# Joining a weight word's low bits by an OR on VectorE, and a first gate step as a rectifier on ScalarE

## The chip, the cores and the metric

The kernel runs on one core of a Trainium2 chip. The metric is the device time of one execution in microseconds (us). A core has five engines that run side by side, each through its own instructions in order: TensorE (PE in the rows, with its weight loads as PEld), VectorE (DVE), ScalarE (ACT), GpSimd (POOL) and SyncE (SP), which issues most DMAs.

## The reference

An attention layer is followed by a feed-forward layer with a piecewise gate. For each of 8 batches and 8 heads (576 tokens, 64 channels):

```
out_d     = softmax(q_d k_d^T / 8) v_d          # q_d, k_d, v_d: means over groups of 4 tokens
out_local = softmax(q k^T / 8 where |i - j| < 4) v
x         = repeat(out_d, 4) + out_local        # 4608 tokens x 512
h         = x @ w_in                            # 512 -> 2048
g         = h where h >= 1, 0 where h <= -1, else (h + 1)^2 / 4
out       = g @ w_out                           # 2048 -> 512
```

The two weight matrices arrive as 64-bit floats: each weight is two 32-bit words, a high one and a low one.

## The kernel before, in words

**Numbers.** Each operand of the feed-forward products is held as two tiles in TensorE's fast 32-bit format: a rounded high part and the rest. A product is then three matmuls: high by high, low part of the weight by high, high by low part of the activations.

**Weights.** `w_in` and `w_out` are cut into 16 blocks each (`i0` to `i15`, `o0` to `o15`; 128 x 512 weights). The kernel makes single precision from the 64-bit words in six pieces per block, in the function `convert`. `c1` (L803, ACT) turns the high word in place: sign and exponent. `c3` (L816, DVE) shifts it left by three into a new tile `m`. `c2` brings down the top three bits of the low word: on ACT (L812) for 24 blocks, on DVE (L810) for the eight odd `o` blocks named in `ON_VECTOR`. `c4` (L819, DVE) adds these bits to `m`; this 32-bit integer addition is built as an instruction of its own that works on 1,024 16-bit halves. `c5` (L822, ACT) rounds `m` to the high part `w[:, 0]`, and `c6` (L826, POOL) subtracts that from `m` for the rest, `w[:, 1]`.

**Stages.** The first 512 tokens are chunk 0. While the first eight head pairs of the attention run, the weights are loaded and converted, and chunk 0 passes both products, all interleaved. From about 155 us on, the weights are there, and the other chunks (384 tokens, later 512) pass with the rest of the attention. The last two chunks use a Strassen scheme.

**Gate.** For a block `f` of 128 hidden channels, TensorE sums `h` in PSUM (`f.s0` to `f.s3`, L847; chunk 0 uses two PSUM banks in turn). The gate has five pieces. `u1` is max(h, -1) + 1 (L869, DVE; in chunk 0 it reads PSUM, later a copy `m` made by ACT at L868). `sq` is the square of half of it (L872, ACT). `u2` is min(max(h, 1), that square) (L875, DVE). `gh` rounds (L881, ACT) and `gl` is the rest (L884, POOL). `m{f}.0` to `m{f}.3` (L902) multiply `gh` and `gl` with block `o{f}` for four token groups.

**What sets the order.** In this first part no scheduler moves anything: the table `ORDER` is a written list of tokens (`i6.c4`, `f4.u1`, `m3.2`, `5.x`), and each engine gets its instructions in the order of these tokens. Tokens such as `5.x` are steps of head pair 5: `sl` and `sp` are the local and the pooled scores on TensorE (L311 to L323, L377), `mx` and `ms` the local maximum and its subtraction on DVE (L334, L353), `x` the sum of both attention outputs on DVE (L541). `x` reads the PSUM tile that the next pair's `sl` then writes. Tiles `m`, `u`, `gh` and `gl` share ten buffers (`temp`), so that a writer can wait for the reader of an old tile.

Of the kernel before, what the change touches and what calls it, by code (L numbers as in the profile page):

```python
# [11 lines left out]
I32 = mybir.dt.int32  # L12
U32 = mybir.dt.uint32
U8 = mybir.dt.uint8
AF = mybir.ActivationFunctionType
ALU = mybir.AluOpType
# [11 lines left out]
NFC = DFF // P  # L28
# [52 lines left out]


WARM = 10
ON_VECTOR = {("o", f) for f in range(1, NFC, 2)}

PIECES = (3, 4, 2, 1)

# [73 lines left out]
def attention_then_ffn(ctx: ExitStack, tc, qT, kT, vw, vp, vq, band, members, w_in, w_out, out):  # L161
    nc = tc.nc
# [625 lines left out]
    raw, weights = {}, {}  # L788
# [6 lines left out]
    def temp(name, kind=F32):  # L795
        return mpool.tile([P, 512], kind, name=name, tag="t512", bufs=10)

    def convert(name, f, piece):

        t = raw[name, f]  # L800
        if piece == 1:
            high = t.bitcast(F32)[:, :, 1]
            nc.scalar.activation(high, high, AF.Prelu, scale=2.0**-112, alpha=-(2.0**32))  # L803
        elif piece == 2:
            raw["low", name, f] = t[:, :, 0]
            if (name, f, "m") in raw and (name, f) not in ON_VECTOR:
                raw["low", name, f] = t.rearrange("p n t -> p (n t)")[:, 0:512]
            low = t.bitcast(U32)[:, :, 0]
            if (name, f) in ON_VECTOR:
                nc.vector.tensor_scalar(raw["low", name, f], low, 2.0**-29, None, op0=ALU.mult)  # L810
            else:
                nc.scalar.activation(raw["low", name, f], low, AF.Copy, scale=2.0**-29)  # L812
        elif piece == 3:
            raw[name, f, "m"] = temp("m")
            mi = raw[name, f, "m"].bitcast(I32)
            nc.vector.tensor_scalar(mi, t[:, :, 1], 3, None, op0=ALU.logical_shift_left)  # L816
        elif piece == 4:
            mi = raw[name, f, "m"].bitcast(I32)
            nc.vector.tensor_tensor(mi, mi, raw["low", name, f], op=ALU.add)  # L819
        elif piece == 5:  # L820
            w = wpool.tile([P, 2, 512], F32R, name=f"w_{name}{f}", tag=f"w{name}{f}")
            nc.scalar.copy(w[:, 0], raw[name, f, "m"])  # L822
            weights[name, f] = w
        else:
            w = weights[name, f]
            nc.gpsimd.tensor_tensor(w[:, 1], raw[name, f, "m"], w[:, 0], op=ALU.subtract)  # L826
# [5 lines left out]
    utiles = {}  # L832
# [25 lines left out]
    def gate(c, f, piece):  # L858

        size = CHUNKS[c][1]  # L860
        h = htiles.get((c, f))
        if piece == "u1":
            utiles[c, f] = temp("u")[:, :size]
            if (c, f) in summed:
                m = utiles["m"] = summed[c, f]
            elif c > 0:
                m = utiles["m"] = temp("m")[:, :size]
                utiles["copied"] = nc.scalar.copy(m, h)  # L868
            nc.vector.tensor_scalar(utiles[c, f], m if c > 0 else h, -1.0, 1.0, op0=ALU.max, op1=ALU.add)  # L869
        elif piece == "sq":  # L870
            u = utiles[c, f]
            nc.scalar.activation(u, u, AF.Square, scale=0.5)  # L872
        elif piece == "u2":
            u = utiles[c, f]
            utiles["last"] = nc.vector.scalar_tensor_tensor(  # L875
                u, utiles["m"] if c > 0 else h, 1.0, u, op0=ALU.max, op1=ALU.min
            )
        elif piece == "gh":
            gh, gl = (temp(x, F32R)[:, :size] for x in ("gh", "gl"))
            gtiles[c, f] = gh, gl  # L880
            nc.scalar.copy(gh, utiles[c, f])  # L881
        else:
            gh, gl = gtiles[c, f]
            nc.gpsimd.tensor_tensor(gl, utiles.pop((c, f)), gh, op=ALU.subtract)  # L884

    def gates(c, f, pieces=GATE):
        with tc.high_priority(offset=100):
            for piece in pieces:
                gate(c, f, piece)
# [170 lines left out]
    with psum("pair") as two, tc.manual_schedule(), ExitStack() as six:  # L1060
# [7 lines left out]
        for token in ORDER:  # L1068
            token, _, spare = token.partition("+")
            spare = int(spare or 0)  # L1070
            token, _, tag = token.partition("@")
            whose, what = token.split(".")
            kind, f = whose[0], whose[1:]
            if kind in "io":
                if what == "ld":
                    load_weights(kind, int(f))
                else:
                    convert(kind, int(f), int(what[1]))
            elif kind == "f":
                c, f = divmod(int(f), NFC)  # L1080
                if not banks:
                    six.close()
                    single(six, ["h0"], ["o0"], ["o1", "o2"], ["h1"], ["o3"])
                if what[1:].isdigit() and what[0] == "s":
                    keep_up(banks["o0"][:, 0:P], spare)
                    product(c, f, int(what[1]))
                else:
                    gate(c, f, what)
            elif kind == "m":
                second_product(0, int(f), int(what))  # L1090
            elif tag:
                ops[int(whose)][what](own[tag], tag, spare)
            elif spare:
                ops[int(whose)][what](spare)
            else:
                ops[int(whose)][what]()
# [162 lines left out]
```

## Time and profile before

| | |
|---|---|
| median of 3 runs | 897.67 us (896.5 to 898.2) |
| span of the profiled execution, from its first to its last instruction | 900.0 us |
| PE busy | 885.3 us (98%) |
| DVE busy | 563.7 us (63%) |
| ACT busy | 467.9 us (52%) |
| POOL busy | 375.0 us (42%) |
| PE's share of the chain that ended last | 84% |

The profiled execution is one more than the three timed ones; what is known of its own time is its span, 2.3 us above the median of the runs. Busy shares are means over the whole span; the stages differ, and a share says nothing of who waits for whom at a given moment. For that, idle time of an engine is listed with the instruction that ended it.

### The profile page before, as it was taken

The page shows a single profiled execution, that of the slowest core. Times are in us where ns is not written, and L with a number is a line of the kernel's source. Part 1 is how long each engine was busy: PE and PEld are TensorE (multiplying, and loading weights), DVE is VectorE, ACT ScalarE, POOL GpSimd, SP SyncE. Part 2 cuts the span into 40 slices and gives each one's busy share as a digit, 9 for nine tenths or more (in the row PEclk, how much of TensorE's full clock was granted, in tenths as well). Part 3 has the DMA queues.
Part 4 walks back from the last instruction along what each step waited for, and adds up shares of the span by engine and source line. Part 5 has one row for each costly group of instructions (what it writes and reads, how often), then busy time and mean ns, then how long its engine had stood idle before and what let it go on. Part 6 is the DMA issues. An engine that isn't in the chain of part 4 may idle for free.

```text
span 900.0 us, 19773 instructions
## 1 busy us (share of the span) xinstructions
PE 885.3 (98%) x7808; PEld 798.0 (89%) x7808; DVE 563.7 (63%) x1077; ACT 467.9 (52%) x1025; POOL 375.0 (42%) x361
## 2 busy tenths in 40 slices
PE   8999899999999999999999999999999999999998
PEld 6687688899999999999999999989999989999997
DVE  6699995766566477566556656665556546754442
ACT  4798675554544545554454454564454444434333
POOL 3166783444343244444432443344444434433232
PEclk9999999999999999999999999999999999999999
DMA  9369311333233233333332343342233212434341
GB/s 344 120 213 319 126 57 53 97 110 128 90 115 115 91 106 116 122 120 116 113 103 89 101 133 103 105 139 92 91 127 106 83 51 83 122 109 141 105 126 53
DMA packets 67884, 106.47 MB, mean 118 GB/s; under 512 B 5808, under 2 KB 33456, under 8 KB 67792
## 3 DMA queue, kind: packets, MB, share of 16 engines
q1 hardware_dynamic: 67648, 105.17, 35.5%
q8 instruction: 61, 1.00, 0.4%
q14 instruction: 31, 0.25, 0.1%
q10 hardware_dynamic: 144, 0.05, 0.0%
HBM read 71.51 MB, written 17.83 MB: 99 GB/s over the span
## 4 chain that ended last, share of the span: by engine, by line
PE 84%; DVE 7%; ACT 4%; issue 3%; POOL 2%; DMA 0%; SPq 0%; DVEq 0%; ACTq 0%; POOLq 0%
PE ffn_o L902 37%; PE ffn_h L847 28%; PE ffn_h L1015 7%; PE score_ps L643 2%; PE turn_ps L771 1%; PE value_ps L667 1%; DVE m L819 1%; PE local_ps L768 1%; PE value_ps L625 1%; DVE m L816 1%; DVE u L869 1%; DVE u L875 1%; POOL gl L884 1%; ACT u L872 1%; DVE sums L924 1%
## 5 line engine op out<-in xcount | busy, mean ns | idle before, releaser
L884 POOL TENSOR_TENSOR gl<-u,gh 128x384 fp32r<-128x384 f32 (+1 forms) x176 | 197.0, 1120 | 400.4 <-ACT gh L881 320.3
L902 PE MATMUL ffn_o<-w_o,gh 128*128 128x512 f32 x1152 | 347.5, 383 | 0.0
L847 PE MATMUL ffn_h<-xh,w_i 128*128 128x384 f32 (+1 forms) x1184 | 301.2, 336 | 2.5 <-POOL w_i L826 2.1
L902 PEld LDWEIGHTS ffn_o<-w_o,gh 128*128 128x128 f32 x1152 | 212.0, 190 | 25.2 <-issue 0.6
L847 PEld LDWEIGHTS ffn_h<-xh,w_i 128*128 128x128 f32 x1184 | 209.5, 189 | 16.9 <-POOL w_i L826 2.9
L902 PE MATMUL ffn_o<-w_o,gl 128*128 128x512 f32 x576 | 218.9, 380 | 0.4 <-POOL gl L884 0.4
L847 PE MATMUL ffn_h<-xl,w_i 128*128 128x384 f32 (+1 forms) x592 | 197.3, 333 | 0.0
L872 ACT ACTIVATE u<-u 128x384 f32<-128x384 f32 (+1 forms) x176 | 97.4, 553 | 133.5 <-DVE u L869 133.5
L881 ACT CAST gh<-u 128x384 fp32r<-128x384 f32 (+1 forms) x176 | 95.3, 542 | 118.8 <-DVE u L875 117.3
L869 DVE TENSOR_SCALAR u<-m 128x384 f32<-128x384 f32 (+1 forms) x160 | 76.1, 476 | 127.3 <-ACT m L868 126.9
L875 DVE SCALAR_TENSOR_TENSOR u<-m,u 128x384 f32<-128x384 f32 (+1 forms) x160 | 103.2, 645 | 78.0 <-ACT u L872 78.0
L902 PEld LDWEIGHTS ffn_o<-w_o,gl 128*128 128x128 f32 x576 | 109.3, 190 | 16.4 <-POOL gl L884 0.8
L847 PEld LDWEIGHTS ffn_h<-xl,w_i 128*128 128x128 f32 x592 | 111.9, 189 | 2.2
L868 ACT COPY m<-ffn_h 128x384 f32<-128x384 f32 (+1 forms) x132 | 63.8, 484 | 51.1 <-PE ffn_h L847 42.4
L720 ACT ACTIVATE sl<-sl 128x640 f32<-128x640 f32 x24 | 17.7, 739 | 55.1 <-POOL sl L694 55.1
L581 POOL TENSOR_TENSOR xl<-x,xh 128x576 fp32r<-128x576 f32 (+4 forms) x32 | 35.3, 1110 | 16.6 <-ACT xh L580 16.6
L826 POOL TENSOR_TENSOR w_o<-m,w_o 128x512 fp32r<-128x512 f32 x16 | 24.1, 1517 | 31.2 <-ACT w_o L822 31.2
L924 DVE SCALAR_TENSOR_TENSOR sums<-sums 128x128 f32<-128x128 f32 (+1 forms) x72 | 33.0, 459 | 1.6
L694 POOL TENSOR_TENSOR sl<-sl,mxl 128x640 f32<-128x640 f32 x24 | 30.2, 1260 | 2.3 <-DVE mxl L693 1.7
L924 DVE SCALAR_TENSOR_TENSOR words<-sums,words 128x512 fp32r<-128x512 f32 x16 | 17.7, 1109 | 17.7 <-ACT words L928 17.7
L826 POOL TENSOR_TENSOR w_i<-m,w_i 128x512 fp32r<-128x512 f32 x16 | 22.6, 1415 | 11.6 <-ACT w_i L822 11.4
L1041 POOL TENSOR_TENSOR m<-both 128x256 f32<-128x256 f32 x14 | 10.7, 765 | 39.0 <-DVE both L1040 33.8
(179 smaller groups left out, 1183.4 us busy)
## 6 DMA issues: line engine op xcount, KB each, us to landing
xh<-kept SPq DMA_DIRECT2D x56, 256.0 KB, 3.8
v<-vw SPq DMA_DIRECT2D x29, 320.0 KB, 4.0
vq_sb<-vq SPq DMA_DIRECT2D x24, 384.0 KB, 3.0
out<-osb SPq DMA_DIRECT2D x36, 256.0 KB, 2.4
raw_i<-w_in SPq DMA_DIRECT2D x16, 512.0 KB, 8.7
raw_o<-w_out SPq DMA_DIRECT2D x16, 512.0 KB, 8.9
kept<-words SPq DMA_DIRECT2D x32, 256.0 KB, 2.6
k_sb<-kT SPq DMA_DIRECT2D x28, 288.0 KB, 3.3
```

Of the source, the lines that this page charges most:

```text
L581: nc.gpsimd.tensor_tensor(xl[:, p, dst], x[:, part], xh[:, p, dst], op=ALU.subtract)
L826: nc.gpsimd.tensor_tensor(w[:, 1], raw[name, f, "m"], w[:, 0], op=ALU.subtract)
L847: ins = nc.tensor.matmul(htiles[c, f], wi[:, wt, cc * P : (cc + 1) * P], turns(xt[:, cc, ts]), start=(cc == 0 and xt is xh and wt == 0), s ...
L868: utiles["copied"] = nc.scalar.copy(m, h)
L869: nc.vector.tensor_scalar(utiles[c, f], m if c > 0 else h, -1.0, 1.0, op0=ALU.max, op1=ALU.add)
L872: nc.scalar.activation(u, u, AF.Square, scale=0.5)
L875: utiles["last"] = nc.vector.scalar_tensor_tensor(u, utiles["m"] if c > 0 else h, 1.0, u, op0=ALU.max, op1=ALU.min)
L881: nc.scalar.copy(gh, utiles[c, f])
L884: nc.gpsimd.tensor_tensor(gl, utiles.pop((c, f)), gh, op=ALU.subtract)
L902: ins = nc.tensor.matmul(o, gt[:, ts], turns(weights["o", f][:, wt, :]), start=f == 0 and n == 0, stop=f == NFC - 1 and n == 2,)
L924: return nc.vector.scalar_tensor_tensor(out, a, 1.0, b, op0=ALU.mult, op1=op)
L1015: ins = nc.tensor.matmul(ps, left(wt, k), right(xt, k), start=not more and k == 0 and wt == xt, stop=k == 1 and xt == 1, skip_group_check= ...
```

## The change

It touches `convert` and `gate` alone. Pieces `c2` and `c3` do nothing any more. In `c4`, a first DVE instruction multiplies the low word by 2 to the power -29 and caps the result at 7, into a new tile `m`. A second one shifts the high word left by three and ORs it with `m`. In chunk 0, `u1` becomes one ACT instruction, relu(h + 1), which reads PSUM. The table `ORDER` stays as it is, so the new instructions stand where the tokens `c4` and `u1` stand.

```
-ON_VECTOR = {("o", f) for f in range(1, NFC, 2)}
...
-        elif piece == 2:
-            raw["low", name, f] = t[:, :, 0]
-            if (name, f, "m") in raw and (name, f) not in ON_VECTOR:
-                raw["low", name, f] = t.rearrange("p n t -> p (n t)")[:, 0:512]
-            low = t.bitcast(U32)[:, :, 0]
-            if (name, f) in ON_VECTOR:
-                nc.vector.tensor_scalar(raw["low", name, f], low, 2.0**-29, None, op0=ALU.mult)
-            else:
-                nc.scalar.activation(raw["low", name, f], low, AF.Copy, scale=2.0**-29)
-        elif piece == 3:
+        elif piece in (2, 3):
+            return
+        elif piece == 4:
             raw[name, f, "m"] = temp("m")
             mi = raw[name, f, "m"].bitcast(I32)
-            nc.vector.tensor_scalar(mi, t[:, :, 1], 3, None, op0=ALU.logical_shift_left)
-        elif piece == 4:
-            mi = raw[name, f, "m"].bitcast(I32)
-            nc.vector.tensor_tensor(mi, mi, raw["low", name, f], op=ALU.add)
+            nc.vector.tensor_scalar(mi, t.bitcast(U32)[:, :, 0], 2.0**-29, 7.0, op0=ALU.mult, op1=ALU.min)
+            nc.vector.scalar_tensor_tensor(
+                mi, t[:, :, 1], 3, mi, op0=ALU.logical_shift_left, op1=ALU.bitwise_or
+            )
...
-            nc.vector.tensor_scalar(utiles[c, f], m if c > 0 else h, -1.0, 1.0, op0=ALU.max, op1=ALU.add)
+            if c == 0:
+                nc.scalar.activation(utiles[c, f], h, AF.Relu, bias=1.0)
+            else:
+                nc.vector.tensor_scalar(utiles[c, f], m, -1.0, 1.0, op0=ALU.max, op1=ALU.add)
```

Three places show what moves. The first is DVE around `i2.c4`, between the maximum (`mxl`) and the subtraction (`sl`) of pair 4; `raw_i2` is the loaded block, `m` the tile that is made of it. Before:

```order
L816 TENSOR_SCALAR m_591<-raw_i2_488 128x512
L556 TENSOR_TENSOR xl_70<-pl_ps_521,xh_69 128x64
L819 ISA m_396<-m_396,raw_i0_299 128x1024
L334 TENSOR_REDUCE mxl_648<-sl_ps_600 128x10
L819 ISA m_591<-m_591,raw_i2_488 128x1024
L353 TENSOR_TENSOR sl_674<-sl_ps_600,mxl_648 128x640
```

Now:

```order
L808 TENSOR_SCALAR m_591<-raw_i0_299 128x512
L809 SCALAR_TENSOR_TENSOR m_591<-raw_i0_299,m_591 128x512
L333 TENSOR_REDUCE mxl_641<-sl_ps_594 128x10
L808 TENSOR_SCALAR m_665<-raw_i2_485 128x512
L809 SCALAR_TENSOR_TENSOR m_665<-raw_i2_485,m_665 128x512
L352 TENSOR_TENSOR sl_669<-sl_ps_594,mxl_641 128x640
```

The first of the two instructions for `i2` has moved from ahead of the maximum to behind it, so two instructions now stand between maximum and subtraction instead of one.

The second place is ACT around `f4.u1`; `u_1015` is the gate tile of `f4`, `ffn_h0` its sum in PSUM, `w_o4` and `w_i6` are casts `c5` of two blocks. Before:

```order
L881 CAST gh_1013<-u_985 128x512
L803 ACTIVATE raw_i8_953<-raw_i8_953 128x512
L812 ACTIVATE raw_i6_828<-raw_i6_828 128x512
L822 CAST w_o4_1038<-m_889 128x512
L872 ACTIVATE u_1034<-u_1034 128x512
L812 ACTIVATE raw_o6_857<-raw_o6_857 128x512
L822 CAST w_i6_1053<-m_1021 128x512
```

Now:

```order
L876 CAST gh_997<-u_969 128x512
L802 ACTIVATE raw_i8_937<-raw_i8_937 128x512
L862 ACTIVATE u_1015<-ffn_h0_697 128x512
L814 CAST w_o4_1017<-m_1009 128x512
L867 ACTIVATE u_1015<-u_1015 128x512
L814 CAST w_i6_1035<-m_1025 128x512
```

The two low-word copies are gone, and the cast of `o4` now stands behind an instruction that needs TensorE's sum of `f4`.

The third place is ACT around `f7.u1`; `u_1229` is the gate tile of `f7`. Before:

```order
L822 CAST w_o8_1221<-m_1175 128x512
L822 CAST w_i10_1228<-m_1191 128x512
L822 CAST w_i9_1234<-m_1202 128x512
L822 CAST w_i8_1241<-m_1136 128x512
L803 ACTIVATE raw_o11_1189<-raw_o11_1189 128x512
L872 ACTIVATE u_1249<-u_1249 128x512
```

Now:

```order
L814 CAST w_o8_1197<-m_1184 128x512
L814 CAST w_i10_1208<-m_1191 128x512
L814 CAST w_i9_1214<-m_1199 128x512
L814 CAST w_i8_1221<-m_1205 128x512
L862 ACTIVATE u_1229<-ffn_h1_710 128x512
L802 ACTIVATE raw_o11_1165<-raw_o11_1165 128x512
L867 ACTIVATE u_1229<-u_1229 128x512
```

The first gate step of `f7` has moved from DVE to behind four casts on ACT, each of which needs a finished `m` from DVE.

## Rows read from the trace of the kernel before

**Rows 1.** Windows: length, busy time of each engine (instructions), granted clock, DMA share, GB/s.

```profile
50.00:100.00 50.00, 47.56 (x354) 39.45 (x352) 48.46 (x69) 45.10 (x78) 36.69 (x25) 1.00 0.62 213
...
250.00:300.00 50.00, 50.00 (x458) 46.05 (x457) 32.71 (x70) 24.41 (x57) 20.26 (x22) 1.00 0.32 104
```

**Rows 2.** Timeline of PE: start, time taken, instruction, idle before it with releaser.

```profile
43.64 0.71 PE L377 MATMUL sp_ps<-kd,first_qd 64*64 64x144 f32 x12 [1.19 <-DVE sl L353]
...
47.71 0.48 PE L847 MATMUL ffn_h<-xh,w_i 128*128 128x512 f32 x1 [0.36 <-POOL w_i L826]
...
68.43 0.38 PE L847 MATMUL ffn_h<-xl,w_i 128*128 128x512 f32 x1
...
75.52 0.48 PE L847 MATMUL ffn_h<-xh,w_i 128*128 128x512 f32 x1 [1.77 <-POOL w_i L826]
...
92.60 0.70 PE L847 MATMUL ffn_h<-xh,w_i 128*128 128x512 f32 x2 [0.29 <-DVE u L875]
...
101.88 0.55 PE L311 MATMUL sl_ps<-band_r,ident_r 128*128 128x384 f32 x2 [2.26 <-DVE x L541]
...
109.13 0.71 PE L377 MATMUL sp_ps<-kd,first_qd 64*64 64x144 f32 x12 [0.75 <-DVE sl L353]
...
121.25 0.48 PE L902 MATMUL ffn_o<-w_o,gl 128*128 128x512 f32 x1 [0.43 <-POOL gl L884]
```

**Rows 3.** Window behind the longest of these waits (columns as in rows 1).

```profile
103.00:107.00 4.00, 4.00 (x23) 3.24 (x17) 4.00 (x6) 3.48 (x7) 1.81 (x2) 0.57 0.55 154
```

**Rows 4.** Groups up to 185 us: count, busy us, mean ns of one, idle before.

```profile
L819 DVE CUSTOM_DVE_ANT_0 m<-m,raw_i 128x1024 uint16<-128x1024 uint16 x16 | 14.6, 926 | 2.3 <-ACT raw_i L812 2.3
...
L812 ACT ACTIVATE raw_i<-raw_i 128x512 int32<-128x512 uint32 x16 | 12.5, 797 | 0.0
L816 DVE TENSOR_SCALAR m<-raw_o 128x512 int32<-128x512 int32 x16 | 11.1, 707 | 0.0
...
L869 DVE TENSOR_SCALAR u<-ffn_h 128x512 f32<-128x512 f32 x16 | 11.0, 689 | 1.8 <-PE ffn_h L847 1.7
L816 DVE TENSOR_SCALAR m<-raw_i 128x512 int32<-128x512 int32 x16 | 10.7, 669 | 0.9 <-ACT raw_i L803 0.9
...
L819 DVE CUSTOM_DVE_ANT_0 m<-m,raw_o 128x1024 uint16<-128x1024 uint16 x8 | 8.1, 1012 | 0.4 <-ACT raw_o L812 0.4
L819 DVE CUSTOM_DVE_ANT_0 m<-raw_o,m 128x1024 uint16<-128x1024 uint16 x8 | 8.0, 997 | 0.0
L812 ACT ACTIVATE raw_o<-raw_o 128x512 int32<-128x512 uint32 x8 | 6.9, 864 | 1.1 <-DVE m L816 1.1
...
L810 DVE TENSOR_SCALAR raw_o<-raw_o 128x512 int32<-128x512 uint32 x8 | 6.2, 780 | 0.0
```

**Rows 5.** Single lines: durations in ns, least/median/most, first and last start.

```profile
L816 DVE TENSOR_SCALAR m<-raw_o x16: 420/514/1454, 27.7 to 131.4; 128x512 int32<-128x512 int32 x16
...
L869 DVE TENSOR_SCALAR u<-ffn_h x16: 672/680/742, 47.3 to 143.6; 128x512 f32<-128x512 f32 x16
...
L924 DVE SCALAR_TENSOR_TENSOR sums<-xh,xl x8: 676/681/693, 730.5 to 781.3; 128x512 f32<-128x512 f32 x8
...
L910 ACT COPY osb<-ffn_o x36: 577/587/602, 153.0 to 896.0; 128x512 f32<-128x512 f32 x36
```

**Rows 6.** Timeline of POOL around 72 us (columns as in rows 2).

```profile
70.05 1.98 POOL L826 TENSOR_TENSOR w_o<-m,w_o 128x512 fp32r<-128x512 f32 x1 [2.27 <-ACT w_o L822]
71.99 1.80 POOL L884 TENSOR_TENSOR gl<-u,gh 128x512 fp32r<-128x512 f32 x1
73.75 1.71 POOL L826 TENSOR_TENSOR w_i<-m,w_i 128x512 fp32r<-128x512 f32 x1
...
75.42 1.29 POOL L826 TENSOR_TENSOR w_o<-m,w_o 128x512 fp32r<-128x512 f32 x1
```

**Rows 7.** Timeline of DVE ahead of pair 5's `x` (columns as in rows 2).

```profile
97.90 1.85 DVE L819 CUSTOM_DVE_ANT_0 m<-raw_o,m 128x1024 uint16<-128x1024 uint16 x1
99.68 1.48 DVE L816 TENSOR_SCALAR m<-raw_i 128x512 int32<-128x512 int32 x1
```

## The prediction

> **What bounds the kernel now.** I read the windows first, then TensorE's own idle time, then the groups of instructions, then the timelines of single engines. The windows show two stages. From 155 us on PE is full: 50.00 of 50 us in the window shown, with DVE at 32.71 and ACT at 24.41 [rows 1]. Between 50 and 100 us all are near full: DVE 48.46, ACT 45.10, PE 47.56. The changed code runs in that early part only (the last of its instructions starts at 143.6 us, rows 5 show it for L869), so its worth is what PE loses there. Idle time of DVE or ACT is worth nothing by itself.
>
> PE's losses can be counted. Seven waits are left once the first products start: 1.19, 0.36, 1.77, 0.29, 2.26, 0.75 and 0.43 us, together 7.05 [rows 2]. Behind the longest, the granted clock falls from full to its lower level (2.4 to 1.2 GHz) for most of 103 to 107 us: a mean of 0.57, so 0.43 x 4 = 1.7 us more [rows 3]. PE had been idle for 2.26 us shortly before it fell. The ceiling of the gain is 7.05 + 1.7 = 8.8 us, 1% of the time, whatever the other engines save. As PE is full behind it, what is saved early should arrive at the end undiminished.
>
> **The engines' sums.** DVE loses 32 shifts (11.1 + 10.7), 32 additions (14.6 + 8.1 + 8.0), eight low-word products (6.2) and 16 gate steps (11.0): 69.7 us [rows 4]. It gains 32 low-word products with a cap and 32 shift-and-OR instructions. The first is priced as L810, same input and output kinds, 0.78 us. The second has no row of its own. Below, an undisturbed two-input instruction of its size takes 0.68 [rows 5]; above, one held up takes 1.85 [rows 7]. I take the mean of the additions it replaces, 30.7 / 32 = 0.96, since it stands in the same places beside the same POOL work. That is 32 x (0.78 + 0.96) = 55.7, so DVE is relieved of 14 us (24 us if every OR took 0.68; burdened by 14 more if every OR took 1.85). ACT loses 24 low-word copies, 12.5 + 6.9 = 19.4 us [rows 4], and gains 16 rectifiers from PSUM at 0.59, as L910 takes [rows 5]: 9.4. It is relieved of 10 us. POOL's list of work is unchanged, and so is PE's.
>
> **Wait by wait.** Fewer us do not mean an earlier start where an instruction waits in line, so each of PE's waits is followed to what ends last there.
>
> At 43.64 PE waits for pair 4's subtraction. The product for `i2` now stands between maximum and subtraction, which it did not: about 0.4 us (L816 undisturbed, rows 5) later. PE reaches its next wait, 47.71, that much later, and of the 0.36 there as much goes. Together a loss of 0.1. Nothing hides it, as there is no PE work between the two.
>
> At 75.52 PE waits for `i6.c6` on POOL, third in a row of three without a gap: `o4.c6`, `f3.gl`, `i6.c6`, begun at 70.05 when ACT had cast `o4` [rows 6]. That cast now stands behind `f4.u1`, which cannot start before PE ends `f4`: 68.43 + 0.38 = 68.81 [rows 2]. With 0.59 for the rectifier and an estimated 0.6 for the cast, an ACT instruction of the same size, POOL starts at 70.0. So ACT's relief is eaten here by its new wait, and behind the waiting rectifier stand the casts of `o4` and `i6`, on which POOL depends. What is left is that the three POOL instructions took 1.98, 1.80 and 1.71 where the next one took 1.29 [rows 6], while DVE's pairs for `o5` and `o6` still run beside them. I take 0.5 of the 1.77 (bounds 0 and 1.77).
>
> The rows show that DVE and POOL hold each other up: L816 takes 420 to 1,454 ns, L869, which reads PSUM, 672 to 742 [rows 5]. The Trainium skill (SBUF — State Buffer, section Who interferes with whom) says that a VectorE instruction with two SBUF inputs, or a one-input one in its two-port mode, and a GpSimd instruction that reads SBUF exclude each other for their whole length, and that one SBUF input outside that mode does not contend. By that rule the 16 gate steps that leave never disturbed POOL, and of the disturbing kind only 8 of 72 go. Then the 0.5 would be about 0, and the sum below 0.5 less; the rows fit the rule.
>
> At 92.60 PE waits for DVE's `f7.u2`. Its `u1` now stands on ACT behind four casts, which wait for five pairs of DVE instructions (`o7`, `o8`, `i10`, `i9`, `i8`). I take the wait to stay as it is, 0 gained: before, the same casts came ahead of `sq`.
>
> At 101.88 PE waits 2.26 us for pair 5's `x`, which came late because DVE was behind: the two instructions just ahead took 1.85 and 1.48 [rows 7]. By then DVE has been spared eight gate steps (5.5 us at 0.69), five L810 (3.9) and two shifts that had run ahead (1.4): some 10 us, of a delay of 2.26. What is late next is `x`'s own input from PE, and three quarters of a block of products lie between that and the wait. I take all 2.26, and with it the clock's 1.7 (bounds 0 and 4.0).
>
> At 109.13 PE waits for pair 6's subtraction; one gate step, one L810 and one shift (1.65 by a disturbed run) leave the stretch between that pair's scores and it. I take all 0.75. At 121.25 PE waits for a `gl`; POOL's work there stays, as do DVE's joins beside it: 0 (bounds -0.8 and 0.43).
>
> Sum: -0.1 + 0.5 + 0 + 2.26 + 1.7 + 0.75 + 0 = 5.1 us. The profiled execution would span 900.0 - 5.1 = 894.9; it stood 2.3 us above the median of the runs, 897.67. So I forecast 897.67 - 5.1 = 892.6 us.
>
> **The rivals.** (A) All waits go: the engines' relief carries everywhere, 8.8 - 0.1 = 8.7 us, 889.0. For it: the relief of DVE is larger than any wait. Against it: 75.52 hangs on ACT's place in line and on POOL.
>
> (B) No change to be measured: DVE stays late at `x` since its pairs are each held up, as the two in rows 7. Then 2.26 and 1.7 stay, and 0.75 + 0.5 - 0.1 = 1.2 us are saved: 896.5. For it: the number of disturbing instructions barely falls, and instructions that ran ahead as `c3` now run in pairs at `c4`, near their users.
>
> (C) Slower: the place is `f7.u1`. Five DVE pairs must end before ACT comes to it, then `sq`, `u2` and PE. At 1.74 us a pair (0.78 + 0.96) they take 8.7 us; at 3.33, the sum of rows 7, they take 16.7, and PE waits 8 us more at 92.60. From 1.74 + 5.1 / 5 = 2.8 us a pair on, the gain elsewhere is gone. At 3.33 it is 897.67 - 5.1 + 8.0 = 900.6. Against it: POOL's next casts come from these same five pairs, so it has little work with which to hold them up.
>
> (D) The OR is not one plain pass but takes as long as the slowest row. Were it 1.85 us each, DVE gains no time at all, which is C's cause or B's.
>
> **How the numbers follow.** Forecast with its own range of 890.5 to 895.5: 0.58. A: 0.12. B (895.5 to 899): 0.20, C with D: 0.10. The range runs from A's 889.0 up to 898.0, which leaves out C and the upper part of B. About 0.2%, 1.8 us, is what a measurement of this kernel can tell from no change: faster means under 895.9, slower above 899.5. Forecast, A and a tenth of B fall below: 0.58 + 0.12 + 0.02, and a little of C's small ends: 0.73. Same 0.17, slower 0.10.
>
> **What would show it.** Right: in the new trace PE's wait for `x` at about 99 us is gone and the clock there is full; PE still waits about 1 us for `i6.c6`, with the rectifier of `f4` starting only when PE ends that block; the products and ORs take 0.4 to 0.7 us alone. `sp` of pair 4 starts 0.3 to 0.4 us later than 43.64, and the window from 155 us on is a shifted copy. Wrong: a new PE wait behind a rectifier, above all at `f7` or `f9`; a PE idle time that brings the clock down at another place; or a gain of more than 8.8 us, for which nothing in the early waits has room.

## The result and the profile after

The changed kernel took 907.38 us (median of 5 runs, 905.39 to 908.47), the kernel before 897.67: a ratio of 1.0082, with an interval of 1.0056 to 1.0109. The forecast was 892.6, the range 889.0 to 898.0. The medians alone differ by 9.7 us, 1.1%; one of the five runs of the kernel before took 902.61. The change made the kernel slower by about 1%, and the prediction was wrong in size and in sign.

The profiled execution took 908.47 us, and its span is 906.6: 1.9 us lie around the span. TensorE (PE) is still the engine that is full (888.7 us busy, 98%). From the start of the 384-token chunk to the end both kernels take the same time: PE's first product of it starts at 144.00 us before and at 150.69 after, and the spans end 756.0 and 755.9 us later. So, as predicted, the difference was made in the first part. What follows is PE's idle time there, as [rows 2] show it before: the timeline of PE in the trace after, the waits of over 0.2 us from 40 us on (start, time taken, instruction, idle before it with releaser).

```profile
44.81 0.71 PE L376 MATMUL sp_ps<-kd,first_qd 64*64 64x144 f32 x12 [1.65 <-DVE sl L352]
...
55.69 0.82 PE L468 MATMUL tp_ps<-ident,sp 128*72 128x128 f32 x6 [0.49 <-DVE sp L419]
...
65.92 0.56 PE L310 MATMUL sl_ps<-band_r,ident_r 128*128 128x384 f32 x2 [0.82 <-DVE x L540]
...
77.21 0.48 PE L839 MATMUL ffn_h<-xh,w_i 128*128 128x512 f32 x1 [0.87 <-POOL w_i L818]
...
85.33 0.48 PE L839 MATMUL ffn_h<-xh,w_i 128*128 128x512 f32 x1 [0.30 <-ACT w_i L814]
...
86.69 0.48 PE L839 MATMUL ffn_h<-xh,w_i 128*128 128x512 f32 x1 [0.88 <-POOL w_i L818]
...
97.93 0.70 PE L839 MATMUL ffn_h<-xh,w_i 128*128 128x512 f32 x2 [2.21 <-DVE u L870]
...
145.66 0.70 PE L839 MATMUL ffn_h<-xh,w_i 128*128 128x512 f32 x2 [3.10 <-DVE u L870]
```

The waits at 101.88, 109.13 and 121.25 are gone, and the one at 75.52 is halved. But there are new ones. At 97.93 the first product of `f9` waits for `u2` of `f7`, whose PSUM bank it takes over: 2.21 us where it was 0.29. At 145.66 the first product of `f15` waits in the same way for `u2` of `f13`: 3.10 us, at a place where PE had not waited at all. Behind both, the granted clock falls, as it did behind one wait before [rows 3]. The windows of the trace after (length, busy time of PE, PEld, DVE, ACT and POOL with instructions, granted clock, DMA share, GB/s):

```profile
99.00:103.00 4.00, 4.00 (x12) 2.94 (x10) 3.93 (x4) 1.95 (x4) 4.00 (x3) 0.57 0.01 4
146.00:151.00 5.00, 5.00 (x17) 4.12 (x16) 4.08 (x9) 3.81 (x12) 2.56 (x2) 0.66 0.00 0
```

For most of each stretch the clock is at the lower of its two levels (1.2 instead of 2.4 GHz). That costs 4 x 0.43 = 1.7 us and 5 x 0.34 = 1.7 us. The place at `f13` alone is worth 3.10 + 1.7 = 4.8 of the 6.6 us between the two spans.

Why is `u2` of `f13` late? First the timeline of DVE in front of it, in the trace after (columns as before):

```profile
135.72 0.85 DVE L808 TENSOR_SCALAR m<-raw_i 128x512 int32<-128x512 uint32 x1
136.60 1.91 DVE L809 SCALAR_TENSOR_TENSOR m<-raw_i,m 128x512 int32<-128x512 int32 x1
138.43 0.51 DVE L808 TENSOR_SCALAR m<-raw_o 128x512 int32<-128x512 uint32 x1
138.98 0.84 DVE L809 SCALAR_TENSOR_TENSOR m<-raw_o,m 128x512 int32<-128x512 int32 x1
139.74 1.57 DVE L808 TENSOR_SCALAR m<-raw_o 128x512 int32<-128x512 uint32 x1
141.34 1.66 DVE L809 SCALAR_TENSOR_TENSOR m<-raw_o,m 128x512 int32<-128x512 int32 x1
142.92 0.60 DVE L385 TENSOR_REDUCE sp_ps<-sp_ps 128x3 f32<-128x432 f32 x1
144.91 0.69 DVE L870 SCALAR_TENSOR_TENSOR u<-ffn_h,u 128x512 f32<-128x512 f32 x1 [1.39 <-ACT u L867]
```

Then ACT over the same time:

```profile
138.54 0.62 ACT L814 CAST w_i<-m 128x512 fp32r<-128x512 f32 x1 [1.97 <-DVE m L809]
139.85 0.62 ACT L814 CAST w_o<-m 128x512 fp32r<-128x512 f32 x1 [0.69 <-DVE m L809]
143.03 0.62 ACT L814 CAST w_o<-m 128x512 fp32r<-128x512 f32 x1 [2.56 <-DVE m L809]
143.56 0.59 ACT L862 ACTIVATE u<-ffn_h 128x512 f32<-128x512 f32 x1
144.18 0.63 ACT L867 ACTIVATE u<-u 128x512 f32<-128x512 f32 x1
```

Three pairs (product, then OR) for `i15`, `o14` and `o15` occupy DVE from 135.72 to 143.0. In the kernel before, the same place held the three additions only, and in its trace they ran from 133.78 to 136.56 (DVE):

```profile
133.78 1.42 DVE L819 CUSTOM_DVE_ANT_0 m<-m,raw_i 128x1024 uint16<-128x1024 uint16 x1
135.12 0.68 DVE L819 CUSTOM_DVE_ANT_0 m<-m,raw_o 128x1024 uint16<-128x1024 uint16 x1
135.72 0.84 DVE L819 CUSTOM_DVE_ANT_0 m<-raw_o,m 128x1024 uint16<-128x1024 uint16 x1
```

ACT's three casts wait for the pairs one by one (1.97, 0.69, 2.56 us). The rectifier (L862) stands behind the third cast, and square and `u2` follow. PE's sums of `f13` had been complete since about 139.

So there were two suspects: the rectifier's place in ACT's line, and the pairs on DVE. Both edits come together in this chain, and the trace alone does not tell which one PE pays for.

### The profile page after: what moved, and what is told of

Read it like the earlier page. It is cut to its first block, busy times and chain, and to the rows that moved or that the text cites. A ratio compares the mean times of both kernels' runs of the same rounds, so it can differ in the third digit from the quotient of the medians.

```text
span 906.6 us, 19727 instructions
## 1 busy us (share of the span) xinstructions
PE 888.7 (98%) x7808; PEld 799.4 (88%) x7808; DVE 559.9 (62%) x1053; ACT 460.0 (51%) x1017; POOL 371.8 (41%) x361
## 4 chain that ended last, share of the span: by engine, by line
PE 85%; DVE 7%; ACT 4%; issue 2%; POOL 1%; ACTq 0%; DVEq 0%; POOLq 0%
PE ffn_o L897 36%; PE ffn_h L839 29%; PE ffn_h L1010 7%; PE score_ps L642 2%; DVE m L808 2%; PE turn_ps L770 1%; PE value_ps L666 1%; DVE m L809 1%; PE local_ps L767 1%; PE pl_ps L525 1%; PE value_ps L624 1%; DVE u L870 1%; ACT u L867 1%; DVE sums L919 1%; DVE u L864 1%
```

## The experiments

Theory 1 is that the rectifier stands behind casts that wait for DVE, and so makes the gate late. Theory 2 is that the product, which now stands at `c4` right ahead of the OR, makes the finished `m` late, on whichever engine the gate step is. Theory 3 came up on the way. Each run's ratio is to runs of the kernel before on the same chip, whose median was 898.41 us in the first four experiments, 898.27 in the next four and 898.73 in the last three. The changed kernel was timed only for the first result, so what an experiment gives back against its 907.38 us is a difference between sessions, between which the kernel before moved by 1.1 us (897.67 to 898.73).

**The OR alone.** The rectifier is undone:

```
-            if c == 0:
-                nc.scalar.activation(utiles[c, f], h, AF.Relu, bias=1.0)
-            else:
-                nc.vector.tensor_scalar(utiles[c, f], m, -1.0, 1.0, op0=ALU.max, op1=ALU.add)
+            nc.vector.tensor_scalar(utiles[c, f], m if c > 0 else h, -1.0, 1.0, op0=ALU.max, op1=ALU.add)
```

> The changed kernel with the first gate step of chunk 0 put back on DVE; the low bits are still joined by the product and the OR, both at token c4. Theory 1 (the rectifier's place in ACT's line, behind casts that wait for DVE, makes the gate late): both long PE waits of the changed kernel, 2.21 us at 97.93 and 3.10 at 145.66, and the clock falls behind them go; about the kernel before or a little under, 893 to 898 us. Theory 2 (the two DVE instructions now stand one behind the other at c4, where one stood, and the last of a row ends late whoever does the gate step): the gate step stands on DVE behind the same pairs, which ended at 94.9 and 143.0; then step 0.69, square 0.62 and u2 0.69 follow, so PE waits still about 1.5 and 2.5 us; 904 to 908 us.

Measured: 908.82 us, ratio 1.0112 (1.0087 to 1.0138), 0.8 us above theory 2's range. The loss is all there without a rectifier. PE waits at the same two places, and the clock falls behind both (0.50 from 100 to 102 us and from 147 to 150); trace of this kernel, timeline of PE:

```profile
98.58 0.70 PE L839 MATMUL ffn_h<-xh,w_i 128*128 128x512 f32 x2 [1.92 <-DVE u L867]
...
146.31 0.70 PE L839 MATMUL ffn_h<-xh,w_i 128*128 128x512 f32 x2 [2.47 <-DVE u L867]
```

The gate step now stands on DVE behind the same pairs. Theory 1 is not needed for the loss.

**The rectifier alone.** The kernel before, with only the last part of the diff:

```
-            nc.vector.tensor_scalar(utiles[c, f], m if c > 0 else h, -1.0, 1.0, op0=ALU.max, op1=ALU.add)
+            if c == 0:
+                nc.scalar.activation(utiles[c, f], h, AF.Relu, bias=1.0)
+            else:
+                nc.vector.tensor_scalar(utiles[c, f], m, -1.0, 1.0, op0=ALU.max, op1=ALU.add)
```

> The kernel before with the first gate step of chunk 0 as a rectifier on ACT, and the weights converted as before (copy, shift, integer addition). Theory 1 (ACT's line): the rectifiers of f7 and f13 are again late behind the casts and PE waits 1 to 3 us at each; 901 to 907 us. Theory 2 (DVE's pairs): in the kernel before the three additions ahead of f13's step ended at 136.6, before PE had ended that block's sums (137.6), and the casts behind them at 137.2, so a rectifier behind them waits for PE alone; DVE loses 11 us of work; no new wait at f13, 894 to 899 us.

Measured: 901.3 us, ratio 1.0028 (1.0011 to 1.0044). In the trace there is no wait for `u2` of `f13`, as theory 2 has it, but the time lies in theory 1's range, and at `f9` PE waits 1.27 us: the rectifier is not free, it costs 2.9 us. The profiled execution was the fastest of the twelve (898.2 us), so this trace does not show all of that cost. A part of it the two experiments on `f0` below show.

**The product early.** The changed kernel, with the product where the shift used to stand:

```
-        elif piece in (2, 3):
+        elif piece == 2:
             return
-        elif piece == 4:
+        elif piece == 3:
             raw[name, f, "m"] = temp("m")
             mi = raw[name, f, "m"].bitcast(I32)
             nc.vector.tensor_scalar(mi, t.bitcast(U32)[:, :, 0], 2.0**-29, 7.0, op0=ALU.mult, op1=ALU.min)
+        elif piece == 4:
+            mi = raw[name, f, "m"].bitcast(I32)
```

> The changed kernel with the product and cap issued at token c3 (where the shift stood), only the shift with OR at c4; rectifier on ACT kept. Theory 2 (DVE's pairs at c4): the three instructions ahead of f13 take about 3 us as in the kernel before instead of 7.3, the wait of 3.10 at f13 and its clock fall go, and most of the one at f7; 893 to 899 us. Theory 1 (ACT's line): the rectifier still stands behind the casts, the losses at f7 and f13 stay for the larger part; 903 to 908 us. Both: the subtraction of pair 4 is 0.4 us earlier than in the changed kernel.

Measured: 900.22 us, ratio 1.0016 (0.9999 to 1.0032), just above theory 2's range. The same instructions, same count, same engine, but one of each pair at an earlier place: 7.2 of the 9.7 us are back (907.38 less 900.22). The timeline of DVE ahead of `u2` of `f13` in this trace:

```profile
132.92 1.69 DVE L811 SCALAR_TENSOR_TENSOR m<-raw_i,m 128x512 int32<-128x512 int32 x1
134.53 1.54 DVE L811 SCALAR_TENSOR_TENSOR m<-raw_o,m 128x512 int32<-128x512 int32 x2
```

Three ORs take 3.2 us where the pairs took 7.3, and PE does not wait there any more. At this place theory 2 holds. What is left in the trace are 1.38 us at `f9` and a wait of 1.88 us at 49.92 with a clock fall behind it, of which more below.

**The gate first.** The changed kernel with two places of `ORDER` rewritten (DVE's order stays):

```
-... 5.ap i10.c4 m5.0 o8.c5 i9.c4 m5.1 i8.c4 i10.c5 ... i8.c5 5.tl@hi1 f7.u1 o11.c1 i9.c6 m6.0 f7.sq
+... 5.ap i10.c4 m5.0 f7.u1 f7.sq o8.c5 i9.c4 m5.1 i8.c4 i10.c5 ... i8.c5 5.tl@hi1 o11.c1 i9.c6 m6.0
...
-... o15.c4 o14.c5 f13.s2 6.xl o15.c5 f13.s3 m12.2 f13.u1 i15.c6 7.sp@hi1 f13.sq
+... o15.c4 f13.s2 6.xl f13.s3 m12.2 f13.u1 i15.c6 7.sp@hi1 f13.sq o14.c5 o15.c5
```

> The changed kernel with two places of the written order changed: f7's rectifier and square stand ahead of the casts of o8, i10, i9 and i8, and f13's rectifier and square ahead of the casts of o14 and o15; DVE's order is the same. Theory 1 (ACT's line): u2 of f7 and f13 find their square ready, both waits fall below 0.5 us and the clock stays up there; 899 to 902 us. Theory 2 (DVE's pairs): u2 still stands on DVE behind the pairs that ended at 94.9 and 143.0, so the wait at f7 goes (u2 at about 95), but the one at f13 only shrinks from 3.10 to about 1.5 us (u2 at 143.5); 903 to 906 us.

Measured: 901.56 us, ratio 1.003 (1.0015 to 1.0045): 5.8 us back, within what theory 1 gave and more than theory 2 did, since the clock falls at neither place any more. The wait at `f9` is gone. At `f15` PE still waits, though rectifier and square are done long before (ACT, then PE, in this trace):

```profile
135.94 0.60 ACT L863 ACTIVATE u<-ffn_h 128x512 f32<-128x512 f32 x1
136.57 0.63 ACT L868 ACTIVATE u<-u 128x512 f32<-128x512 f32 x1
```

```profile
140.97 0.70 PE L840 MATMUL ffn_h<-xh,w_i 128*128 128x512 f32 x2 [1.70 <-DVE u L871]
```

`u2` stands on DVE behind the pairs, and that is the part of the wait that no order of ACT can take away. The rest was ACT's: so the pairs are the cause, and with the rectifier behind the casts ACT passes their lateness on.

**Three products early.** To pin the place, the product stands at `c3` for `i15`, `o14` and `o15` only:

```
+EARLY = {("i", 15), ("o", 14), ("o", 15)}
...
-        elif piece in (2, 3):
+        elif piece == 2 or (piece == 3 and (name, f) not in EARLY):
             return
...
```

> The changed kernel with the product at token c3 for three blocks only, i15, o14 and o15, the three pairs that stand ahead of u2 of f13 on DVE. Theory 2: the wait of 3.10 us at f15's first product and the clock fall behind it (1.8 us) go, everything before stays; 907.4 less 4.9 is 902.5, range 901.5 to 904. Theory 1 (the rectifier's place in ACT's line): the casts still stand ahead of it and the wait stays above 1.5 us; 905 to 908.

Measured: 903.44 us, ratio 1.0054 (1.0039 to 1.0068); 3.9 us back from three instructions of 32, somewhat under the 4.9 expected, and inside theory 2's range. PE's wait at `f15` is gone; the one of 2.21 us at `f9` stays.

**The kernel before, again.** No edit, a second profile.

> The kernel before, unchanged, profiled a second time. The prediction counted PE's wait of 2.26 us for x and the clock fall behind it (1.7 us) as losses of every execution. Theory A (they belong to the kernel): the second trace shows them again, its span is about 900. Theory B (they belong to that one execution, whose span of 900.0 is 4.2 us above what 897.67 us less the 1.9 us around a span give): the wait at x is under 0.5 us, the clock stays up, the span is 894.5 to 897.

Measured: 898.88 us, span 897.1 (0.1 above theory B's range), mean granted clock 1.000 (0.997 in the trace of the first profile). The timeline of PE in this second trace, all waits of over 0.2 us from 40 us on:

```profile
44.09 0.71 PE L377 MATMUL sp_ps<-kd,first_qd 64*64 64x144 f32 x12 [1.19 <-DVE sl L353]
...
48.17 0.48 PE L847 MATMUL ffn_h<-xh,w_i 128*128 128x512 f32 x1 [0.36 <-POOL w_i L826]
...
75.78 0.48 PE L847 MATMUL ffn_h<-xh,w_i 128*128 128x512 f32 x1 [1.62 <-POOL w_i L826]
...
92.91 0.70 PE L847 MATMUL ffn_h<-xh,w_i 128*128 128x512 f32 x2 [0.33 <-DVE u L875]
...
105.88 0.71 PE L377 MATMUL sp_ps<-kd,first_qd 64*64 64x144 f32 x12 [1.01 <-DVE sl L353]
...
120.75 0.77 PE L456 MATMUL tl_ps<-ident,sl 128*128 128x128 f32 x5 [0.35 <-ACT ap L485]
```

The wait of 2.26 us for `x` is not there, and the clock stays up. Theory B holds: these 3.96 us belonged to the one execution that was profiled first. For the clock, the timed runs say the same: a loss of 1.7 us lowers a run's mean granted clock by 0.002, and of the 72 runs of the kernel before that stand beside the experiments only five show 0.998 or less (899.80 to 902.19 us). Which instructions of DVE are held up differs between the two: the shift that had taken 1.61 us at 93.19 in the first trace took 0.57 at 93.44 in the second.

**Early product, gate step on DVE.** The kernel of the early product without the rectifier (the edit of the first experiment on top of it).

> The kernel before with the OR alone, its product and cap at token c3 and the shift with OR at c4; the first gate step stays on DVE. Theory 2 (what cost was the two instructions in a row at c4): from the 900.2 us of the early product with rectifier, less the 2.9 us that the rectifier alone cost (901.3 against 898.4), 897.3; range 896 to 899. Rival (the rectifier is worth something once the pairs are split, since it takes 11 us from DVE): this comes out above 900.2, since DVE has those 11 us again.

Measured: 897.84 us, ratio 0.9994 (0.9984 to 1.0004). The OR, with its product placed early, is worth no difference that can be measured. At `f9` PE still waits 1.16 us in this trace, so the rectifier is not the only cause of the 1.38 us that the early product leaves there.

**Early product, gate first.** Both edits, with the rectifier:

> The changed kernel with the product at token c3 and, in the written order, the rectifier and square of f7 and f13 ahead of the casts that stood before them. With the product early only PE's wait of 1.38 us for u2 of f7 was left of the new ones. Theory 1 (a rest of the loss is ACT's line): that wait goes, 900.2 less 1.4 is 898.8; range 897 to 899.5. Theory 2 alone (DVE's pairs were all of it, the rest is noise between executions): 900 to 901, no change.

Measured: 899.56 us, ratio 1.0014 (1.0006 to 1.0022). The time lies between the ranges of both theories. PE's wait at `f9` is gone as theory 1 has it, but the time fell only by 0.7, and by the ratios of the two kernels (1.0016 and 1.0014) that is no difference: in this trace the clock is at its lower level from 50 to 53 us, behind a wait of 1.88 us at 49.52. That wait stood in the traces of the rectifier alone and of the early product too, and led to theory 3: taking `f0`'s gate step off DVE lets DVE's next instructions run into POOL's subtraction for `i1`. In the trace of the rectifier alone, DVE's shifts, POOL's subtraction, and PE's wait for it:

```profile
47.04 0.42 DVE L816 TENSOR_SCALAR m<-raw_o 128x512 int32<-128x512 int32 x1
47.38 0.42 DVE L816 TENSOR_SCALAR m<-raw_i 128x512 int32<-128x512 int32 x1
```

```profile
46.12 2.80 POOL L826 TENSOR_TENSOR w_i<-m,w_i 128x512 fp32r<-128x512 f32 x1
```

```profile
48.98 0.48 PE L847 MATMUL ffn_h<-xh,w_i 128*128 128x512 f32 x1 [1.88 <-POOL w_i L826]
```

**The rectifier, but not for `f0`.** The kernel of the rectifier alone with one step back on DVE:

```
-            if c == 0:
+            if c == 0 and f > 0:
                 nc.scalar.activation(utiles[c, f], h, AF.Relu, bias=1.0)
             else:
-                nc.vector.tensor_scalar(utiles[c, f], m, -1.0, 1.0, op0=ALU.max, op1=ALU.add)
+                nc.vector.tensor_scalar(utiles[c, f], m if c > 0 else h, -1.0, 1.0, op0=ALU.max, op1=ALU.add)
```

> The kernel before with the rectifier on ACT for f1 to f15 and f0's step on DVE; weights converted as before. The rectifier alone, for all sixteen, cost 2.9 us (901.3 against 898.4). Theory 3: PE's wait for i1's low part falls from 1.88 back to 0.36 us and the clock behind it stays up; most of the 2.9 goes, 898 to 899.5. Rival (cost spread over all steps, above all at f7, where PE waited 1.27 us): 900.5 to 901.5.

Measured: 899.44 us, ratio 1.0007 (0.9995 to 1.0019). One step of sixteen gave back 1.9 of the 2.9 us; the intervals of the two ratios still overlap (1.0011 to 1.0044 without it), and the experiment after this one settles it. In this trace DVE runs the gate step at 47.85 and the shifts from 48.45 on, POOL's subtraction takes 1.29 us, and PE's wait is 0.37:

```profile
46.93 1.29 POOL L826 TENSOR_TENSOR w_i<-m,w_i 128x512 fp32r<-128x512 f32 x1
```

```profile
48.27 0.48 PE L847 MATMUL ffn_h<-xh,w_i 128*128 128x512 f32 x1 [0.37 <-POOL w_i L826]
...
96.26 0.70 PE L847 MATMUL ffn_h<-xh,w_i 128*128 128x512 f32 x2 [1.27 <-DVE u L878]
```

The 1.27 us at `f9` stay. By this trace that is ACT's line at `f7`, theory 1's share of the rectifier's cost: DVE sits idle for 2.50 us before `u2` until ACT's square is there. No run with the weights converted as before took it away. In this trace the clock fell, too, from 77 to 81 us, behind a wait of 1.96 us at 76.50, and 7 of the 12 runs show a mean clock of 0.998 or less.

**All three mends.** Early product, gate first at `f7` and `f13`, `f0`'s step on DVE (the edits above together).

> The kernel with early product and reordered f7 and f13 (899.56 us), with the gate step of f0 alone put back on DVE. Theory 3 (with f0's step off DVE, DVE's next shifts or products start 0.7 us earlier and run into POOL's subtraction for i1, which took 2.80 instead of 1.28 us in the trace of the rectifier alone, so that PE waits 1.88 us instead of 0.36 and its clock falls behind the wait in some executions): that wait returns to 0.36, the clock stays up; 1.5 us and in most executions the 1.7 of the clock are saved, 896.5 to 898. Rival (the rectifier's cost lies elsewhere on ACT, spread over all sixteen): one step of sixteen moves nothing, 899 to 900.

Measured: 896.14 us, ratio 0.9965 (0.9952 to 0.9978): faster than both kernels, than the one before by 0.35%, and 0.4 us below theory 3's range. The same kernel with `f0`'s step on ACT had 1.0006 to 1.0022, so the worth of that one step is clear of the noise. All seven runs show a mean clock of 0.999 or more; with the step on ACT 11 of 12 showed 0.998 or less. Not shown is that this gain needs the change: the kernel before was not run with `f7` and `f13` rewritten in `ORDER`. Its waits at the two places, 0.33 us and none in the second profile, leave that little room. PE's waits in this trace, all over 0.2 us from 40 us on:

```profile
44.46 0.71 PE L377 MATMUL sp_ps<-kd,first_qd 64*64 64x144 f32 x12 [1.19 <-DVE sl L353]
...
48.53 0.48 PE L842 MATMUL ffn_h<-xh,w_i 128*128 128x512 f32 x1 [0.36 <-POOL w_i L821]
...
75.88 0.48 PE L842 MATMUL ffn_h<-xh,w_i 128*128 128x512 f32 x1 [1.42 <-POOL w_i L821]
...
90.83 0.48 PE L900 MATMUL ffn_o<-w_o,gl 128*128 128x512 f32 x1 [0.31 <-POOL gl L882]
```

**`i2` later.** On top of that, `ORDER` puts `i2`'s steps later:

```
-... i0.c5 i2.c4 3.xh 4.ms i0.c6 ... 3.xl i2.c5 4.sp@hi1 ... 4.ex i2.c6 3.yl ... i1.c5 f0.s3 ... i1.c6 4.e1
+... i0.c5 3.xh 4.ms i2.c4 i0.c6 ... 3.xl 4.sp@hi1 ... 4.ex 3.yl ... i1.c5 i2.c5 f0.s3 ... i1.c6 i2.c6 4.e1
```

> As the kernel with early product, reordered f7 and f13 and f0's step on DVE, and in the written order the OR of i2 behind pair 4's subtraction, its cast behind i1's, its POOL subtraction behind i1's. Theory (PE's wait of 1.19 us at pair 4's pooled scores is DVE's instruction for i2 between maximum and subtraction, 0.68): the wait falls to about 0.5 and i1's low part comes no later, so 0.6 to 1 us less than that kernel, 895.5 to 897. Rival (PE only reaches its next wait, for POOL, earlier): no change from it.

Measured: 895.89 us, ratio 0.9966 (0.9954 to 0.9978), no difference from 896.14, though inside the theory's range too. The wait at pair 4 fell from 1.19 to 0.72, but a new one of 0.49 came at 50.91, for DVE and not for POOL. The rival was right in that nothing is gained.

## Why the prediction was wrong

PE's losses in the three traces from 40 us on, in us, added up from the timelines and the windows (the 5.16 include a wait of 0.15 at 48.67, too short for the list above):

| | before, first profile | before, second | after |
|---|---|---|---|
| waits up to 95 us, without `f9` | 3.32 | 3.17 | 5.16 |
| `f9` for `u2` of `f7` | 0.29 | 0.33 | 2.21 |
| 95 to 125 us | 3.44 | 1.36 | 0 |
| `f15` for `u2` of `f13` | 0 | 0 | 3.10 |
| clock | 1.7 | 0 | 3.4 |
| sum | 8.8 | 4.9 | 13.9 |
| span | 900.0 | 897.1 | 906.6 |

Against the first profile the sum after is larger by 5.1 us and the span by 6.6, against the second by 9.0 and 9.5. Of the rest against the first, 0.7 us lie in the first 9 us (PE's first L342 at 7.84 and, as L341, at 8.55). By the traces, the three steps of the prediction in the next three paragraphs make 12.4 of the 14.8 us between forecast and measurement.

**"I take all 2.26, and with it the clock's 1.7."** This term held 3.96 of the 5.1 us. The wait did go, but it was a loss of the profiled execution, not of the kernel: the second trace lacks it. The number that could have warned stood in the text: the span lay 2.3 us above the median of the runs. Some 1.9 us lie around a span, so that execution took about 901.9, 4.2 us more than the median. The forecast subtracted from the median a loss that the median did not hold. With this term at 0 the forecast would have been 896.5, rival B's figure, and still on the wrong side.

**"I take the wait to stay as it is, 0 gained" at 92.60.** This step failed, and it cost 2.21 - 0.29 + 1.7 = 3.6 us. Rival C named the place and the mechanism, but let them decide only from 2.8 us a pair, taking 1.74 as no change. The five pairs took 8.4 us in the trace after (86.44 to 94.8), as forecast. What the step missed is that before, only the additions stood at that place: the shifts had run ahead, but for one, so 8.4 us replaced five additions of 4.0 us together (0.82 + 0.67 + 2.53), in the trace before:

```profile
85.17 0.82 DVE L819 CUSTOM_DVE_ANT_0 m<-raw_o,m 128x1024 uint16<-128x1024 uint16 x1
...
86.25 0.67 DVE L819 CUSTOM_DVE_ANT_0 m<-m,raw_o 128x1024 uint16<-128x1024 uint16 x1
...
87.30 2.53 DVE L819 CUSTOM_DVE_ANT_0 m<-m,raw_i 128x1024 uint16<-128x1024 uint16 x3 [0.38 <-ACT raw_i L812]
```

Moving an instruction from an earlier token to its partner's does not change a sum, but adds its whole length to the chain at the later place. The early product, which undoes just that, shows it at `f13`, where the wait goes altogether. At `f9` it takes away 0.8 of the 1.9 us and the clock fall. Of the rest, the gate first at `f7` takes away all, but 1.16 us stand there with the gate step on DVE, too: how they divide between the ORs' length and ACT's line stays open.

**The list of waits ended at 121.25.** The step "each of PE's waits is followed to what ends last there" followed the waits that PE had, and not the places where it only just did not wait. At `f15` PE had no wait in [rows 2], so the prediction passed over it; there the largest loss came, 3.10 + 1.7. Three products early gave 3.9 us of it back. Here the pairs took 7.3 / 3 = 2.4 us each, near C's 2.8.

**The engines' sums** were near. The groups of the trace after, up to 190 us:

```profile
L809 DVE SCALAR_TENSOR_TENSOR m<-raw_o,m 128x512 int32<-128x512 int32 x16 | 18.5, 1154 | 0.6
L809 DVE SCALAR_TENSOR_TENSOR m<-raw_i,m 128x512 int32<-128x512 int32 x16 | 16.7, 1046 | 0.6
L808 DVE TENSOR_SCALAR m<-raw_o 128x512 int32<-128x512 uint32 x16 | 13.3, 832 | 0.0
L808 DVE TENSOR_SCALAR m<-raw_i 128x512 int32<-128x512 uint32 x16 | 12.2, 762 | 0.0
```

```profile
L862 ACT ACTIVATE u<-ffn_h 128x512 f32<-128x512 f32 x16 | 9.5, 592 | 4.5 <-PE ffn_h L839 4.5
```

DVE gained 60.7 us against 55.7 forecast: product 0.80 against 0.78, OR 1.10 against 0.96. Rival D is out: the shortest OR took 0.69 us, like one plain pass. The rectifier took 0.59 as forecast, 9.5 us against 9.4. One side figure was added up wrongly: with every OR at 0.68 the relief is 23 us, not 24. DVE had 9 us less to do (forecast 14) and ACT 10 us less, as forecast, and the kernel was slower: the sums were near and said nothing of the time.

**The small terms.** At 43.64 the wait grew by 0.46 (forecast about 0.4), and 0.21 of it went at the next one. At 75.52 it shrank by 0.9 (taken: 0.5; by the rule that the prediction cites there, about 0), in the way forecast: the rectifier of `f4` waits for PE until 71.50, POOL starts at 72.68, and its three instructions take 4.6 us instead of 5.5. At 109.13 all went, as taken, and the second profile has that wait too (1.01). At 121.25 the 0.43 went (taken: 0). New small waits at 55.69, 65.92, 85.33 and 86.69, 2.49 us together, were not foreseen; they are gone with the early product (with the gate step on DVE, 0.86 and 0.46 are left at two of the places).

**What the relief of DVE was worth.** The prediction took fewer instructions on DVE as a gain or nothing. At `f0` it was a loss: in the trace of the rectifier alone DVE ran the next two shifts at 47.04, where the gate step would have stood, beside POOL's subtraction, which took 2.80 us instead of 1.29. The Trainium skill (SBUF — State Buffer, Who interferes with whom) says that a VectorE instruction with at most one SBUF input and outside its two-port mode does not contend with GpSimd. The gate step, which reads PSUM, is one: by that rule it was cover for POOL's work, and the trace agrees (1.29 with it). The prediction had cited this rule, and used it only to price a relief as small, not to see that the next instruction in line would come in its place. In the changed kernel itself this did no harm: the shifts are gone there, DVE starts none of its conversion steps beside that subtraction, which takes 1.29 us at 47.33 with the rectifier on ACT, and PE's wait is 0.15 us. So it is the next instruction that costs, not the rectifier as such.

What stays open: how much of the pairs' length at `f13` (three of six instructions took 1.57 to 1.91 us, where others of their kind took 0.5 to 0.85) is POOL's work beside them. No run took that work away.

## What to carry to other kernels

Before a loss in a trace is counted as a gain, see that the typical run has it: add what lies around a span, compare with the median, and profile a second time if one execution stands above it. Where two instructions are fused or brought together, follow the one that moved: a step that ran early in another's shadow lengthens the chain at its new place, even if the engine's total falls, and the places to look at are those where the critical engine nearly waits, too. An instruction that is taken away lets the next one start earlier, and that one may disturb a neighbour that the old one left alone.

## What was not expected of the hardware

POOL's subtraction grew by 1.5 us (2.80 against 1.29) from two DVE shifts of 0.42 us each that began after it had begun, so it lost more than their length. PE's wait confirms the size: 1.88 against 0.37. In the two other traces with `f0`'s step on ACT and two products in the shifts' place it took 2.80 us as well. The prediction has such instructions exclude each other for their whole length; here POOL's, which had begun first, did not keep the shifts out: they took no longer than the shortest of their kind (420 ns, [rows 5]).

The clock did not fall behind every wait of a size. Behind 2.21 us it stood at 0.57 from 99 to 103 us after the change; in the trace of the three early products, with the same wait of 2.21 us at 97.06, it stayed at its upper level:

```profile
98.00:103.00 5.00, 5.00 (x65) 4.04 (x64) 4.93 (x4) 3.71 (x7) 4.86 (x4) 1.00 0.13 19
```

Two waits of 1.88 us behaved the same way: at 49.92 in the trace of the early product the clock fell, at 48.98 in that of the rectifier alone it did not. These are traces of different kernels, but the runs of one kernel divide, too, by their mean granted clock. With the rectifier alone, 8 of 12 runs show 0.998 or less and took 900.83 to 903.59 us; the other four took 898.20 to 900.16. With the early product it is again 8 of 12, 899.98 to 902.94 us against 898.12 to 899.00. (With the rectifier for all but `f0`, 7 of 12 show it and were not slower.) So a clock loss behind a wait is one that some executions have and others don't. The spread of the kernel before (896.25 to 902.77 us) is for the most part something else: its 44 runs with a mean clock of 1.000 span the whole of it. What that is, the runs do not show.
